# Clock products from a constant, and two products moved ahead of a wait: the two ends of a TensorE-bound cross network

## The chip, the cores and the metric

One core of a Trainium2 chip. The metric is the device time of one execution in microseconds. Most numbers below are of two kinds: the **time** of a run, and the **span** that the profile of one execution shows from first to last instruction.

## The reference, cut to what matters

```
B, F, D, L = 16384, 26, 16, 6          # Din = 416
x = x0
for l in range(L):
    proj = einsum('bd,de->be', x, ws[l]) + bs[l]
    x = x0 * proj + x                   # x0 [16384, 416], ws [6, 416, 416], all bf16
```

## The kernel before

The rows are in 8 groups of 2048. A group lies in SBUF transposed, features on partitions: three tiles of 128 features and a tail of 32. TensorE multiplies, ScalarE takes the sum out of PSUM and adds the bias (L398), VectorE multiplies by x0 (L407) and adds x (L412). A helper `add` records every operation with what it reads and writes and sets semaphores from that; each engine's list is in the order of the calls.

Ahead of the first data, products that nobody reads keep TensorE busy. They are there to have its clock open sooner: in e5, without them, it opened at 9.34 us, in the profile of after at 4.54. I call them clock products, and 128 columns of one a unit:

```
def keep_busy(n, b):
    while n > 0:
        m = min(n, 4)
        add("pe", lambda h, m=m: h.matmul(
            bank(b, n=m * P).rearrange("p (m c) -> p m c", m=m), ones[:, :],
            ones[:, :].unsqueeze(1).broadcast_to([P, m, P]), start=True, stop=True),
            reads=["ones"], writes=[("ps", b)])
        n -= m
keep_busy(22, 7)          # before the first transposes
...                       # keep_busy(2, 3) between them, keep_busy(5, 3) after them
```

The last job (last group, last layer) works with rows on partitions, so that its output can be stored as it is: four row blocks kk, each of four chunks j, each chunk three products of 416 columns (`nat_full`, L868), one product of the 32-row tail (`nat_rows`, L912) and one of the bias (L917). ScalarE copies a chunk out (L923), VectorE multiplies (L929) and adds the residual (L935), and one store per block goes out. The residual of the last tile is still being made when this starts, and TensorE transposes it (`turn_last`, L879):

```
a0, a1, a2, a3 = bka = take(NJ)
b0, b1, b2, b3 = take(NJ)
bks = {0: bka, 1: [b0, b3, b1, a0], 2: [a1, a2, a3, b2], 3: [b0, b3, b1, a0]}
store(LAST - 1, 0, 2)                  # output of the last but one group,
store(LAST - 1, 2, NJ)                 # two stores of 832 KB
for j in range(NJ):
    nat_full(0, j, bks[0][j], True, (0, 1))
turn_tails(b0)
nat_rows(0, bks[0], False)
turn_last(0, b1)
turned_out(0, b1)
for j in range(NJ):
    if j == 2:
        turn_last(2, b2)
    nat_full(0, j, bks[0][j], False, (2,))
    nat_out(0, j, bks[0])
...
for kk in range(1, KK):
    nat_rows(kk, bks[kk])
    for j in range(NJ):
        nat_full(kk, j, bks[kk][j], False)
        nat_out(kk, j, bks[kk])
        ...                            # nat_mul, nat_add on VectorE, nat_store
```

## Time and profile before

| | before |
|---|---|
| time, median of 3 runs | 475.43 us (475.24 to 475.45) |
| time and span of the profiled run | 477.81 us, 476.0 us |
| TensorE busy | 470.3 us (99%) |
| first real product | 6.46 us |
| last store issued | 473.58 us |

The prediction shows the lines of the page, of the chain and of the timeline.

### The profile page before, as it was taken

To read this page: it belongs to the slowest core of one execution; us is meant where nothing else is said; L and a number is where in the kernel's file an instruction comes from. 1 tells how busy PE (TensorE), PEld (TensorE's weight loads), DVE (VectorE), ACT (ScalarE), POOL (GpSimd) and SP (SyncE) were. 2 spreads that over 40 slices of the span, in tenths; PEclk is the share of its full clock that TensorE was granted. 3 is DMA by queue.
4 is the path that set the end of the run, shared out by engine and by line. 5 is a ranking of instruction groups with operands and counts; after the bars stand their busy time and mean duration, and the time that the engine had idled before them with its cause. 6 is when DMAs were issued, how large, how long until landed. Compare 5 with 4: busy or idle time off the path is not lost.

```text
span 476.0 us, 8464 instructions
## 1 busy us (share of the span) xinstructions
PE 470.3 (99%) x3407; PEld 200.9 (42%) x3407; DVE 404.2 (85%) x699; ACT 342.0 (72%) x372; POOL 6.3 (1%) x15
## 2 busy tenths in 40 slices
PE   8999999999999999999999999999999999999996
PEld 4434444654444444444444444444444444444442
DVE  1798888888888888898889869988888888888897
ACT  3677777777777777777777777777777777777776
POOL 1000000000000000000000000000000000001000
PEclk9999999999999999999999999999999999999999
DMA  8986830650001398469409940890001029125899
GB/s 223 171 173 143 185 88 1 110 113 1 19 16 30 65 240 147 67 134 239 111 12 170 240 102 10 175 289 2 1 1 35 0 56 232 34 45 101 222 175 288
DMA packets 138651, 53.18 MB, mean 112 GB/s; under 512 B 112362, under 2 KB 138100, under 8 KB 138612
## 3 DMA queue, kind: packets, MB, share of 16 engines
q1 hardware_dynamic: 138456, 52.54, 49.9%
q8 instruction: 26, 0.43, 0.4%
q14 instruction: 13, 0.11, 0.1%
q10 hardware_dynamic: 156, 0.11, 0.1%
HBM read 5.97 MB, written 13.63 MB: 41 GB/s over the span
## 4 chain that ended last, share of the span: by engine, by line
PE 96%; DMA 2%; ACT 1%; DVE 1%; SPq 0%; issue 0%; DVEq 0%
PE ps L471 78%; PE ps L492 7%; PE ps L513 7%; PE ps L868 1%; PE ps L486 1%; DMA wm<-in_ws_dram 1%; ACT tw L398 1%; PE ps L504 1%; PE ps L592 1%; DMA ot<-x 1%; DVE tw L407 0%; PE ps L879 0%; ACT x L923 0%; DVE x L929 0%; DVE x L935 0%; PE ps L912 0%
## 5 line engine op out<-in xcount | busy, mean ns | idle before, releaser
L398 ACT ACTIVATE tw<-ps,bias 128x1024 bf16<-128x1024 f32 (+1 forms) x295 | 299.8, 1071 | 119.5 <-PE ps L492 81.1
L471 PE MATMUL ps<-x,wm 128*128 128x512 bf16 (+1 forms) x1755 | 380.9, 373 | 0.5 <-DMA wm<-in_ws_dram 0.5
L471 PEld LDWEIGHTS ps<-x,wm 128*128 128x128 bf16 x1755 | 165.3, 98 | 210.0 <-issue 29.3
L407 DVE TENSOR_TENSOR tw<-tw,x 128x1024 bf16<-128x1024 bf16 (+1 forms) x285 | 192.7, 684 | 51.8 <-ACT tw L398 51.2
L412 DVE TENSOR_TENSOR x<-tw,x 128x1024 bf16<-128x1024 bf16 (+1 forms) x285 | 182.6, 681 | 0.0
L492 PE MATMUL ps<-x,w 32*128 32x512 bf16 x512 | 39.2, 379 | 0.0
L513 PE MATMUL ps<-x,wm 128*32 128x512 bf16 x564 | 33.0, 380 | 0.0
L438 ACT ACTIVATE ts<-ps,bias 128x512 bf16<-128x512 f32 x47 | 28.8, 701 | 0.0
L442 DVE TENSOR_TENSOR x<-ts,x 128x512 bf16<-128x512 bf16 x47 | 18.7, 419 | 3.9 <-DMA x<-x 3.8
L513 PEld LDWEIGHTS ps<-x,wm 128*32 128x32 bf16 x564 | 13.8, 96 | 17.6 <-issue 5.3
L492 PEld LDWEIGHTS ps<-x,w 32*128 32x128 bf16 x512 | 7.8, 92 | 26.9 <-issue 26.4
L440 DVE TENSOR_TENSOR ts<-ts,x 128x512 bf16<-128x512 bf16 x47 | 18.6, 419 | 0.0
L602 DVE COPY x<-ps 128x512 bf16<-128x512 bf16 x5 | 2.0, 423 | 10.7 <-PE ps L592 10.7
L712 POOL COPY ost<-ot 128x512 bf16<-128x512 bf16 x6 | 4.8, 805 | 424.3 <-DMA ot<-x 424.3
L868 PE MATMUL ps<-wm,x 128*128 128x416 bf16 x48 | 9.5, 340 | 0.0
L604 ACT ACTIVATE x<-ps 128x512 bf16<-128x512 bf16 x7 | 3.8, 595 | 7.4 <-PE ps L592 7.4
L923 ACT ACTIVATE x<-ps 128x416 bf16<-128x416 f32 x16 | 7.8, 526 | 1.6 <-PE ps L868 1.5
L868 PEld LDWEIGHTS ps<-wm,x 128*128 128x128 bf16 x48 | 4.3, 98 | 4.2 <-issue 1.0
L504 PE MATMUL ps<-x,w 32*32 32x512 bf16 x188 | 5.9, 374 | 0.0
L486 PE MATMUL ps<-x,w 32*32 32x512 bf16 x208 | 5.6, 385 | 0.0
L929 DVE TENSOR_TENSOR x<-x,x 128x832 bf16<-128x832 bf16 (+1 forms) x10 | 4.9, 502 | 0.6 <-ACT x L923 0.4
L935 DVE TENSOR_TENSOR x<-x,x 128x832 bf16<-128x832 bf16 (+1 forms) x9 | 4.7, 540 | 0.2
(41 smaller groups left out, 35.4 us busy)
## 6 DMA issues: line engine op xcount, KB each, us to landing
out_dram<-ost SPq DMA_DIRECT2D x6, 1664.0 KB, 7.0
x<-x SPq DMA_DIRECT2D x24, 96.0 KB, 2.1
wm<-in_ws_dram SPq DMA_DIRECT2D x6, 312.0 KB, 3.4
x<-in_x_dram SPq DMA_DIRECT2D x8, 208.0 KB, 4.8
x<-in_x_dram SPq DMA_DIRECT2D x4, 416.0 KB, 8.3
out_dram<-ost SPq DMA_DIRECT2D x2, 832.0 KB, 5.5
x<-x SPq DMA_DIRECT2D x22, 64.0 KB, 2.0
out_dram<-x SPq DMA_DIRECT2D x3, 416.0 KB, 4.1
```

Source lines behind the costliest of these rows:

```text
L398: add("act", lambda h, a=a, w=w, b0=b0: h.activation(tw[r][:, a * CH:(a + w) * CH], psum[:, b0 * CH:(b0 + w) * CH], ACT_F.Identity, bias=b ...
L407: add("dve", lambda h, a=a, e=e: h.tensor_tensor(tw[r][:, a * CH:e * CH], tw[r][:, a * CH:e * CH], x0s[s0][:, i * GC + a * CH:i * GC + e * ...
L412: add("dve", lambda h, a=a, e=e: h.tensor_tensor(xs[so][:, i * GC + a * CH:i * GC + e * CH], tw[r][:, a * CH:e * CH], src(i, a, e), ALU.ad ...
L438: add("act", lambda h: h.activation(ts[r][:, :], bank(b), ACT_F.Identity, bias=bias[:, 3, l:l + 1], scale=1.0), reads=[("ps", b), "bias"], ...
L440: add("dve", lambda h: h.tensor_tensor(ts[r][:, :], ts[r][:, :], x03, ALU.mult), reads=[("ts", r)] + tok0, writes=[("ts", r)], release=True)
L442: add("dve", lambda h: h.tensor_tensor(x3s[so][:, :], ts[r][:, :], res, ALU.add), reads=[("ts", r)] + rtok, writes=[("x3", so), ("x3", so, ...
L471: add("pe", lambda h, t=t, j=j, k=k, w=w: h.matmul(bank(banks[j])[:, k * w:(k + 1) * w], wm[l][:, t, ecols], src(t, j, j + 1)[:, k * w:(k ...
L486: add("pe", lambda h, q=q, j=j, r=r, c=c, o=o: h.matmul(psum[o, banks[j] * CH:(banks[j] + 1) * CH], w3[l][q, i * P + c * T32:i * P + (c + ...
L492: add("pe", lambda h, q=q, j=j, r=r: h.matmul(bank(banks[j]), w3[l][q, ecols], src[q, :], start=first and not inner, stop=not first and no ...
L504: add("pe", lambda h, l=l, b=b, s3=s3, ri=ri, qi=qi, ro=ro, qo=qo: h.matmul(psum[qo, b * CH:(b + 1) * CH], w3[l][qi, NT * P:D], s3[qi, :], ...
L513: add("pe", lambda h, t=t, j=j, src=src, l=l, b=b, ro=ro, qo=qo: h.matmul(psum[qo, b * CH:(b + 1) * CH], wm[l][:, t, NT * P:D], src(t, j, ...
L868: add("pe", lambda h, t=t: h.matmul(bank(b, n=D), xcol(t, j, kk), wm[l][:, t, :], start=(first and t == 0), stop=(not first and t == NT - 1)),
```

## The change

The intent: begin the clock products sooner, by reading a constant that is written at 0.30 us, before the queues begin at 0.73 to 0.80, instead of a tile that GpSimd must fill first (0.73 to 0.93 us), and use the time gained for three more units; and use the wait for the last residual tile for two products of the second row block.

```
 def keep_busy(n, b):
+    one = nc.const_aps.tensor(1.0, [P, CH], BF16)
     while n > 0:
         m = min(n, 4)
         add("pe", lambda h, m=m: h.matmul(
-            bank(b, n=m * P).rearrange("p (m c) -> p m c", m=m), ones[:, :],
-            ones[:, :].unsqueeze(1).broadcast_to([P, m, P]), start=True, stop=True),
-            reads=["ones"], writes=[("ps", b)])
+            bank(b, n=m * P), one[:, 0:P], one[:, 0:m * P], start=True, stop=True), writes=[("ps", b)])
         n -= m
-keep_busy(22, 7)
+keep_busy(25, 7)
...
 nat_rows(0, bks[0], False)
+nat_full(1, 1, bks[1][1], True, (0, 1))
 turn_last(0, b1)
...
 for kk in range(1, KK):
-    nat_rows(kk, bks[kk])
+    begun = (1,) if kk == 1 else ()
+    nat_rows(kk, bks[kk], begun=begun)     # no fresh start for a chunk that has begun
     for j in range(NJ):
-        nat_full(kk, j, bks[kk][j], False)
+        nat_full(kk, j, bks[kk][j], False, (2,) if j in begun else range(NT))
```

More of the change, by code (lines that the diff above doesn't have):

```diff
@@ L907, in turn_tails, with nat_rows @@
             j += n
-    def nat_rows(kk, bks, first=True):
+    def nat_rows(kk, bks, first=True, begun=()):
         for j in range(NJ):
@@ L912, in nat_rows @@
             add("pe", lambda h, j=j, q=q, r=r: h.matmul(
-                bank(bks[j], n=D), x3col(j, kk), w3[l][q, :], start=first, stop=False, tile_position=(r * T32, 0)),
+                bank(bks[j], n=D), x3col(j, kk), w3[l][q, :], start=first and j not in begun, stop=False, tile_position=(r * T32, 0)),
                 reads=tok3 + [("w3", l, r)], writes=[("ps", bks[j])])
```

## The prediction

The clock estimate: that the doubling stays at 10.3 us, worth 0, against rival 1 (20%), that it comes at about 6.9 us, for a time of about 474. The 6.9 us is 10.28 less 3.41 us. The forecast's sum is 475.43 - 0.1 (tail) - 0 (head) = 475.33 us, less some 0.2 for the 20% of a gain near 1.2, so 475.2, in a range of 474.2 to 475.6.

> **What bounds the kernel now.** I read the page's busy shares, then the chain that ended last, then the timeline of the first 13 us and of the last 17 us, because the change touches only those two ends.
>
> ```profile
> PE 470.3 (99%) x3407; PEld 200.9 (42%) x3407; DVE 404.2 (85%) x699; ACT 342.0 (72%) x372; POOL 6.3 (1%) x15
> PE 96%; DMA 2%; ACT 1%; DVE 1%; SPq 0%; issue 0%; DVEq 0%
> ```
>
> TensorE sets the pace: 99% busy and 96% of the chain. The change removes no product between 14 and 459 us, so it can only move the two ends. The start of the chain, in order of time (start, duration, what):
>
> ```profile
> 1.65 4.67 DMA wm<-in_ws_dram
> 6.33 0.14 issue
> 6.46 2.72 PE ps L471 x6
> 9.18 1.97 PE ps L592 x24
> 11.16 1.29 PE ps L471 x6
> ```
>
> The first real products wait for the first weight matrix, which lands at 6.32 us. Six products of 512 columns then take 2.72 us (453 ns each), the next six 1.29 us (215 ns each): TensorE ran at half rate first. The 24 transposes of 128 columns between them take 1.97 us; 12 at about 107 ns and 12 at about 56 ns give that, so the rate doubled at about 10.3 us (estimate: 8.97 us, the first transpose, plus 12 x 0.107). The row of granted clock shows 9 in every slice and does not show this. The clock products (the page's L572) stand ahead of it:
>
> ```profile
> 0.73 0.20 POOL L522 MEMSET ones<- 128x128 bf16 x1 [0.29 <-POOLq L1003]
> 0.98 0.13 PEld L572 LDWEIGHTS ps<-ones 128*128 128x128 bf16 x2 [0.98 <-POOL ones L522]
> 0.99 2.53 PE L572 MATMUL ps<-ones 128*128 128x512 bf16 x6 [0.99 <-POOL ones L522]
> 3.37 0.56 PEld L592 LDWEIGHTS ps<-ident,x 128*128 128x128 bf16 x6 [0.55 <-DMA x<-in_x_dram]
> ```
>
> They wait for the memset of ones (0.73 to 0.93) and end as the first rows land. At the tail, VectorE:
>
> ```profile
> 461.94 0.42 DVE L407 TENSOR_TENSOR tw<-tw,x 128x512 bf16<-128x512 bf16 x1
> 462.28 0.75 DVE L412 TENSOR_TENSOR x<-tw,x 128x512 bf16<-128x512 bf16 x2
> 466.39 0.59 DVE L929 TENSOR_TENSOR x<-x,x 128x832 bf16<-128x832 bf16 x1
> 467.02 0.59 DVE L935 TENSOR_TENSOR x<-x,x 128x832 bf16<-128x832 bf16 x1
> 467.53 0.59 DVE L929 TENSOR_TENSOR x<-x,x 128x832 bf16<-128x832 bf16 x1
> 468.15 0.59 DVE L935 TENSOR_TENSOR x<-x,x 128x832 bf16<-128x832 bf16 x1
> ```
>
> The chain calls the tail TensorE's, but here VectorE runs nearly without a gap from 466.39 us on: starts lie 0.63, 0.51, 0.62 and 0.58 us apart while one operation lasts 0.59. That matters below.
>
> [...]I expect no slower weight load (0.15 us now); this trace does not show it.
>
> **The change part by part.**
>
> *Clock products, start.* The constant is written at 0.30 us, before the start barrier; the other queues begin at 0.73 to 0.80 us. So I put the first product at about 0.75 instead of 0.99: 0.24 us earlier. *Clock products, number.* 25 units of 128 columns instead of 22. A 512-column product starts every 0.427 us (weight loads at 1.39, 1.82, 2.24, 2.67), so a unit is 0.107 us: 25 x 0.107 = 2.67, end 0.75 + 2.67 = 3.42 us; before, 0.99 + 22 x 0.107 = 3.34. The first transposes move from 3.37 to about 3.42. They are off the path: the weights land at 6.32 whatever happens. Direct worth: 0.
>
> *The clock.* [...] So most probably the doubling stays at 10.3 us and is worth 0. If it did come at 6.9 us: of six products from 6.46, one is cold and five run at 0.216, saving about 5 x 0.21 = 1.05 us; 12 cold transposes save 12 x 0.051 = 0.6. The sum 1.65 us is an upper estimate, since the rows of the later chunks are still landing until about 8.5 us and the copies out of PSUM lie between.
>
> *The tail.* Two products of the second row block (bank b3) move ahead of the transposes. Bank b3 is the last tile's own fourth bank: ScalarE frees it only when its fourth eviction (L398, four from 459.31, 2.41 us long) ends at 461.72. On TensorE, the rows' products issue at 461.33; in the later row blocks the next full product follows 0.28 us after them with nothing to wait for (463.95 to 464.23). So the transposes at 461.61 were not late at all, though the profile puts 0.34 us of idle to the add before them. The true gap is from 461.61 + 4 x 0.056 = 461.83 to 462.08 (0.25 us, the add of the second chunk), and another before 462.75.
>
> Worked forward: pair at 461.77 and 461.95 (0.176 us apart: 12 of them start over 1.94 us, 11 steps); eight transposes 462.13 to 462.58; two products to 462.95; transposes of chunks 2 and 3 (data at 462.75 and 463.08) at 462.95 and 463.17; last two products from 463.41 instead of 463.32. So block 0 ends 0.09 us **later**: of 0.35 us put in, 0.26 fell into gaps. Block 1 then has 10 full products instead of 12: 0.35 us off. Net for TensorE, 0.26 us earlier into blocks 2 and 3.
>
> *What follows it.* ScalarE: block 0's third copy-out starts 0.37 us after its product, 463.69 now, 463.80 after; then the fourth, the 1.03 us copy of the turned chunks (464.51) and block 1's two, all back to back; so VectorE's multiply at 466.39 moves to about 466.49. From there VectorE needs 0.63 + 0.51 us per pair. Seven more starts (0.63, 0.51, 0.62, 0.51, 0.62, 0.51, 0.62) and 0.51 to the next put the first single multiply of the last block at 466.49 + 4.53 = 471.02, where it starts at 470.99 now. The second single multiply starts at 471.41 now, waiting for ScalarE's copy that begins at 470.86; that copy now comes 0.26 us earlier, so it follows at about 471.33. The rest hangs on it: 0.08 us earlier. **Sum of the tail: about 0.1 us gained**, against 0.35 us of product time moved.
>
> **The rivals.**
>
> 1. [...] 20%.
> 2. *TensorE alone sets the tail*: then 0.26 us would be gained, 475.15. For: the chain's tail is mostly PE L868. Against: VectorE's gapless starts.
> 3. *The wait for bank b3 takes the place of the wait for the tile*: if the transposes are held longer than I worked out, every later copy slips, and the end comes up to 0.2 us later, 475.6. For: the bank is freed 0.11 us after the point where TensorE wanted to go on. Against: the gaps at 461.83 and 462.4 absorb most.
> 4. *Broadcast reads are slow or upset the clock*[...]. Nothing in the profile speaks for it; the ones tile held the same values. 3%.
>
> **Range and chances.** The main path is 475.43 - 0.1 = 475.33. Weighing in 20% for a gain near 1.2 us takes off some 0.2 in the mean; I say 475.2. The three runs before spread over 0.21 us, so the upper end is 475.6; the lower end 474.2 holds part of the clock's case. Two per cent is 9.5 us, more than five times the largest effect here, so "within 2%" is nearly certain.
>
> **What would show it.** Right: the first clock product at about 0.75 us; the first weight product still at 6.46, the six products from there still 2.7 us; the moved pair at about 461.77, released by ScalarE's L398; block 0's last pair about 0.1 us later; block 1 with 10 products; VectorE without gaps from 466.5 us, and the end some 0.1 us earlier. Wrong: if the 24 transposes or the six products take half, the clock opened earlier, and the gain is over 1 us; if VectorE shows waits for ScalarE through blocks 2 and 3, TensorE led and the gain is 0.26; if the moved pair starts after 462.0, it costs.

## The result, and the profile after

| | before | after |
|---|---|---|
| median of 6 runs in the same rounds | 475.44 us (475.13 to 476.41) | 475.75 us (475.00 to 477.76) |
| ratio, 95% interval | | 1.0009 (0.9989 to 1.0029) |
| span of the profiled run | 476.0 us | 473.7 us |

Ratios here are the mean time of one kernel's runs over that of the other's of the same rounds, so not quite the ratio of the medians. The median lies 0.15 us above my range. And the two spans say the opposite of the two medians: the profiled run of after is 2.3 us **shorter**.

The page of after, the line of busy time and the chain's shares by engine:

```profile
PE 462.3 (98%) x3354; PEld 200.1 (42%) x3408; DVE 404.1 (85%) x699; ACT 341.9 (72%) x372; POOL 6.1 (1%) x15
PE 93%; ACT 3%; DVE 2%; issue 1%; DMA 1%; DVEq 0%
```

TensorE lists fewer products (3354) than before (3407) although the change removes none: a trace can miss some, and the busy sum with them. So I go by positions in time. The timeline of the start after (start, length, engine, line):

```profile
0.77 2.83 PE L573 MATMUL ps<-const-bfloat16-1.0 128*128 128x512 bf16 x7 [0.77 <-PEq L1004]
3.39 0.85 PE L591 MATMUL ps<-ident,x 128*128 128x128 bf16 x6
...
4.24 0.65 PE L591 MATMUL ps<-ident,x 128*128 128x128 bf16 x6
...
6.06 1.46 PE L471 MATMUL ps<-x,wm 128*128 128x512 bf16 x6 [0.52 <-ACT x L603]
```

The products start at 0.77 as intended. The second group of six transposes takes 0.65 us instead of 0.85, so the clock opened in the middle of it, at about 4.5 us (on record 4.54), and the first six real products take 1.46 us where the profile before had 2.72. The first real product also starts sooner, at 6.06 us instead of 6.46. That looks like a gain of two microseconds, and by the prediction's own signs of being wrong it would be one of over 1 us; the timed runs show none of it. Either something gives it back, or the two profiles are not of the same kind of run.

The tail after, VectorE and the moved pair (L867 here is L868 before):

```profile
459.66 0.53 PE L867 MATMUL ps<-wm,x 128*128 128x416 bf16 x2 [0.26 <-ACT tw L398]
...
464.36 0.59 DVE L928 TENSOR_TENSOR x<-x,x 128x832 bf16<-128x832 bf16 x1
464.98 0.59 DVE L934 TENSOR_TENSOR x<-x,x 128x832 bf16<-128x832 bf16 x1
465.49 0.58 DVE L928 TENSOR_TENSOR x<-x,x 128x832 bf16<-128x832 bf16 x1
466.11 0.59 DVE L934 TENSOR_TENSOR x<-x,x 128x832 bf16<-128x832 bf16 x1
```

The pair waits 0.26 us for ScalarE's last eviction, and VectorE then runs without gaps, at steps of 0.62 and 0.51 us up to the single operations of the last block, as predicted. The tail is measured below from ScalarE's copy (L710, after: L709) to the issue of the last store; before and after:

```profile
458.78 0.63 ACT L710 ACTIVATE ost<-ot 128x512 bf16<-128x512 bf16 x1 [0.57 <-DMA ot<-x]
473.58 0.38 ACTq L942 DMA_DIRECT2D out_dram<-x  x1
```

```profile
456.66 0.63 ACT L709 ACTIVATE ost<-ot 128x512 bf16<-128x512 bf16 x1 [0.73 <-DMA ot<-x]
471.33 0.38 ACTq L941 DMA_DIRECT2D out_dram<-x  x1
```

473.58 - 458.78 = 14.80 us and 471.33 - 456.66 = 14.67 us: the last store is issued 0.13 us sooner.

### The profile page after: what moved, and what is told of

Its sections match the earlier page's. It is cut to its first block, busy times and chain, and to the rows that moved or that the text cites. A ratio compares the mean times of both kernels' runs of the same rounds, so it can differ in the third digit from the quotient of the medians.

```text
span 473.7 us, 8412 instructions
## 1 busy us (share of the span) xinstructions
PE 462.3 (98%) x3354; PEld 200.1 (42%) x3408; DVE 404.1 (85%) x699; ACT 341.9 (72%) x372; POOL 6.1 (1%) x15
## 4 chain that ended last, share of the span: by engine, by line
PE 93%; ACT 3%; DVE 2%; issue 1%; DMA 1%; DVEq 0%
PE ps L471 77%; PE ps L492 7%; PE ps L513 6%; ACT tw L398 2%; PE ps L486 1%; DVE x L928 1%; DVE x L934 1%; PE ps L573 1%; PE ps L504 1%; ACT x L922 1%; DMA ot<-x 1%; PE ps L591 0%; ACT x L603 0%; ACT x L888 0%; DVE x L601 0%
## 5 line engine op out<-in xcount | busy, mean ns | idle before, releaser
L471 PE MATMUL ps<-x,wm 128*128 128x512 bf16 (+1 forms) x1701 | 372.1, 371 | 6.1 <-issue 3.7
L492 PE MATMUL ps<-x,w 32*128 32x512 bf16 x512 | 39.2, 379 | 0.0
L492 PEld LDWEIGHTS ps<-x,w 32*128 32x128 bf16 x512 | 7.8, 92 | 26.9 <-issue 26.4
L867 PE MATMUL ps<-wm,x 128*128 128x416 bf16 x48 | 9.7, 340 | 0.3 <-ACT tw L398 0.3
L867 PEld LDWEIGHTS ps<-wm,x 128*128 128x128 bf16 x48 | 4.2, 98 | 4.8 <-issue 1.0
```

The lines of the kernel that those rows point to most:

```text
L471: add("pe", lambda h, t=t, j=j, k=k, w=w: h.matmul(bank(banks[j])[:, k * w:(k + 1) * w], wm[l][:, t, ecols], src(t, j, j + 1)[:, k * w:(k ...
L492: add("pe", lambda h, q=q, j=j, r=r: h.matmul(bank(banks[j]), w3[l][q, ecols], src[q, :], start=first and not inner, stop=not first and no ...
L867: add("pe", lambda h, t=t: h.matmul(bank(b, n=D), xcol(t, j, kk), wm[l][:, t, :], start=(first and t == 0), stop=(not first and t == NT - 1)),
```

## The experiments

Sixteen runs were made (e1 is the kernel before, e2 and e12 are the changed kernel). Theory one: both kernels have early and late runs, by when the clock opens; the change gains a tenth in the tail and the first medians are scatter. Rivals: one of the two parts costs 0.3 us.

### 1 to 4: both kernels again, and each part alone (one chip)

Edits: none; none (changed kernel); the `keep_busy` part of the diff alone; the `nat_full` part alone.

> The kernel before, unchanged, against itself. Theory (two kinds of run): the profiled run of before (477.81 us, span 476.0) was of a late kind in which TensorE's clock opened at about 10.3 us; its timed runs at 475.4 were of an early kind. So times cluster at 475.2 to 475.6 with a rare 477.5 to 478, ratio 1.000, and a profile that falls in the early kind shows a span near 473.6 and the first six weight products in about 1.5 us, not 2.7. Rival (the profile alone is slow): all profiles have a span of 476 and six products in 2.7 us, whatever the timed runs say.

> The changed kernel again. Theory (two kinds, tail worth 0.1): fast kind at 475.3 to 475.6, ratio to before 0.9995 to 1.0000 where both are of the early kind; a late run now and then near 477.8. Rival (the change costs): 475.7 to 475.9 again, ratio 1.0005 to 1.0010 in runs of the early kind.

> Only the clock products' part of the change (constant source, 25 units). Theory: in runs of the early kind nothing, 475.4, ratio 1.0000 within 0.0005; only the share of late runs may change. Rival (the head costs): 475.8, ratio 1.0008, because the first transposes start later or the clock opens later in the typical run.

> Only the two moved products. Theory: 0.1 us less than before, 475.3, with VectorE gapless from the first multiply of the second row block on. Rival (TensorE leads): 475.15. Rival (the moved pair holds up the transposes): 475.6 or more.

| | median, us | lowest to highest | span of the profile |
|---|---|---|---|
| kernel before in the same rounds (11 runs) | 476.03 | 475.25 to 477.65 | |
| e1_before (6) | 475.67 | 475.60 to 475.98 | 473.9 |
| e2_after (7) | 475.51 | 475.39 to 478.24 | 476.4 |
| e3_head (6) | 475.76 | 475.60 to 477.56 | 473.9 |
| e4_tail (6) | 475.70 | 475.43 to 476.65 | 473.8 |

All four ratios have intervals that include 1; the upper ends are 1.0001 (e2) to 1.0014 (e3). Taken alone, the medians of e1, e3 and e4 lie above what I had expected and those of e3 and e4 near their rivals' numbers, but so does the kernel before in the same rounds, at 476.03; the ratios, 0.9984 to 0.9995, speak for no loss. Now it is the kernel before that has the short profile and the changed kernel the long one. The start of the kernel before in the run e1:

```profile
4.17 0.72 PE L592 MATMUL ps<-ident,x 128*128 128x128 bf16 x6
...
5.65 1.46 PE L471 MATMUL ps<-x,wm 128*128 128x512 bf16 x6
```

The kernel before has an early kind too, with the clock open before the first weights (six products in 1.46 us). And the changed kernel in the run e2, a late one:

```profile
3.39 0.51 PE L591 MATMUL ps<-ident,x 128*128 128x128 bf16 x6
...
4.55 0.45 PE L573 MATMUL ps<-const-bfloat16-1.0 128*128 128x512 bf16 x2
...
7.08 2.72 PE L471 MATMUL ps<-x,wm 128*128 128x512 bf16 x6 [2.08 <-DMA wm<-in_ws_dram]
```

Six transposes in 0.51 us: here the clock was open at 3.4 us already, earlier than in any other profile. Then the weights came late, TensorE stood idle for 2.08 us, and the six real products ran at half rate again (2.72 us, in e1 1.46): the clock had closed. So a late run comes about in two ways, by opening late (the profile before) or by opening early and closing in the wait.

The kept traces also record when the granted clock changed. `prof e2_after --windows` gives its mean over a stretch (the number before the last two):

```profile
3.40:6.80 3.40, 1.60 (x24) 1.00 0.98 272
6.90:10.20 3.30, 3.12 (x12) 0.50 1.25 260
10.30:13.00 2.70, 2.63 (x33) 1.00 0.91 187
```

By the record the clock of e2 was full from 3.40 to 6.82 us, at half to 10.23 us, and full again: two steps of 3.41 us. In the records of the first two profiles the time from the first opening to the last closing is 464.21 us (before) and 467.63 us (after), 136.0 and 137.0 times 3.413 us. So in these three profiles the changes of the clock lie whole steps of 3.41 us apart. The first opening came at 3.40 to 5.44 us in 15 profiles and at 9.34 to 10.38 us in three (before, e5, e12): the steps do not begin with the kernel, and the three with the later opening are late runs. The clock is not all of the scatter: the first real product began between 5.65 us (e1) and 7.08 us (e2), mostly as the weights landed, and that moves early runs too.

What this settles: the 2.3 us between the first two profiles are not the change's. The rival that a part costs 0.3 us is not borne out in these rounds: the whole change is at 475.51 us in the median, the kernel before at 476.03.

### 5 to 7: take the clock products away, fill the wait, move a copy

e5 takes all clock products out of the changed kernel; e6 fills the wait for the weights; e7 moves the copy (L709) that ScalarE does ahead of the last tile's evictions.

```
e5:  +    n = 0                     # in keep_busy
e6:  -    keep_busy(5, 3)           +    keep_busy(14, 3)
e7:  -    spread("act")             +    spread("pool")
```

> The changed kernel with every clock product taken out (results unchanged). Theory (the time's scatter is the clock's opening): nothing keeps TensorE busy before the first weights at about 6.1 us, so the clock opens only around 10 us or later in every run: all runs of the late kind, 477.5 to 478.5, none near 475.5; the profile shows the first six weight products in 2.7 us. Rival (the clock products do not matter, the late kind is something else): the same mix as the changed kernel, mostly 475.5.

> The changed kernel with 14 units instead of 5 in the last group of clock products, so that TensorE idles less before the first weights (one profile of the changed kernel had the clock open at 3.4 us and closed again in 2.1 us of waiting for the weights). Theory: early runs unchanged at 475.5, within 0.1; no late run near 478, or fewer. Rival (more clock products only delay): all runs 0.3 to 1 us later.

> The changed kernel with the copy that waits for a DMA ahead of the last tile's evictions moved from ScalarE to GpSimd. ScalarE idles 0.6 to 0.8 us there and then copies for 0.63 us. If ScalarE held up the tail: about 1 us less. My reading: VectorE is the one that is nearly full there (its last tile's operations start at once after the tile before), so only some 0.2 us: 475.3 in early runs, and the stretch from the last tile's first eviction to the last store's issue changes accordingly. Rival: GpSimd's copy slows VectorE's operations beside it, and nothing or a loss comes out.

| | median, us | lowest to highest | ratio, 95% interval |
|---|---|---|---|
| kernel before in the same rounds (9) | 475.99 | 475.67 to 476.56 | |
| e5_noclock (5) | 477.90 | 476.85 to 478.46 | 1.0037 (1.0024 to 1.0051) |
| e6_bridge (5) | 475.60 | 475.35 to 475.91 | 0.9990 (0.9978 to 1.0003) |
| e7_pool (5) | 475.56 | 475.50 to 475.65 | 0.9989 (0.9977 to 1.0002) |

Without clock products TensorE's start is, in its profile:

```profile
3.37 1.56 PE L592 MATMUL ps<-ident,x 128*128 128x128 bf16 x12 [3.37 <-DMA x<-in_x_dram]
...
5.72 2.72 PE L471 MATMUL ps<-x,wm 128*128 128x512 bf16 x6 [0.51 <-DMA wm<-in_ws_dram]
```

The six products are at half rate. The fastest of the five runs is 0.3 us above the slowest of the kernel before, and the medians are 1.9 us apart. Two runs, 476.85 and 477.00, are below the 477.5 I had expected. The first of them is the profiled one: its clock opened at 9.34 us (10.38 in the profile before), and its weights let TensorE start at 5.72 us (6.46). The clock's opening does make most of the late kind, and the clock products of either kernel buy about 2 us in most runs. For e6, five runs are too few to say that late runs are gone.

e7 met its rival. The two additions of the tile before the last took 1.29 us in the changed kernel and, beside GpSimd's copy, this long in e7 (the first line is the changed kernel's):

```profile
456.57 1.29 DVE L412 TENSOR_TENSOR x<-tw,x 128x1024 bf16<-128x1024 bf16 x2
456.39 1.70 DVE L412 TENSOR_TENSOR x<-tw,x 128x1024 bf16<-128x1024 bf16 x2
```

GpSimd's copy began at 456.55 and showed 1.00 us, so it ran beside these additions, which took 0.41 us longer than without it; by what mechanism, no trace shows. So, it seems, VectorE gave back what ScalarE gained: from the last tile's row products (L492) to the last store's issue e7 takes 17.18 us and the changed kernel 17.19.

### 8 and 9: is it VectorE that keeps half of the tail's gain?

In both kernels without the additions of row blocks 1 and 2 (wrong result):

```
             elif j % 2:
                 nat_mul(kk, j - 1)
-                nat_add(kk, j - 1)
```

> Wrong result on purpose: the kernel before without the additions of row blocks 1 and 2, so that VectorE has room in the tail. From the ScalarE copy ahead of the last tile's evictions to the issue of the last store the kernel before takes 14.80 us and the changed one 14.67 in every profile. Theory (VectorE takes over the tail): here TensorE leads, and this stretch stays near 14.75 to 14.80 since TensorE led it before too.

> Wrong result on purpose: the changed kernel without the additions of row blocks 1 and 2. Theory (VectorE takes over the tail and keeps half of the gain): the stretch from the ScalarE copy ahead of the last tile's evictions to the issue of the last store falls to about 14.5, that is 0.25 to 0.3 below the same edit of the kernel before, instead of 0.13 below. Rival (the waiting pair costs the other half, VectorE is innocent): the difference stays 0.13.

The measure is again the stretch from ScalarE's copy ahead of the last evictions to the issue of the last store (ACTq). The two ran on different chips. It is steadier than any time: 14.80 us in all three profiles with the old tail and complete work (before, e1, e3), 14.67 in all six with the new one (after, e2, e4, e5, e6, e12). Without the additions, before and after:

```profile
457.22 0.63 ACT L710 ACTIVATE ost<-ot 128x512 bf16<-128x512 bf16 x1 [0.76 <-DMA ot<-x]
472.03 0.38 ACTq L942 DMA_DIRECT2D out_dram<-x  x1
```

```profile
457.22 0.63 ACT L709 ACTIVATE ost<-ot 128x512 bf16<-128x512 bf16 x1 [0.65 <-DMA ot<-x]
471.73 0.38 ACTq L941 DMA_DIRECT2D out_dram<-x  x1
```

472.03 - 457.22 = 14.81 and 471.73 - 457.22 = 14.51: 0.30 us apart instead of 0.13. So VectorE does keep the other 0.17 us, as predicted. But look at the ends: from the copy to the end of the span both take 17.18 us (474.4 - 457.22). The last store leaves 0.30 us earlier, and the program ends at the same moment. That was not in any of my theories.

### 10 to 12: a later copy, and the changed kernel a third time

e10 puts the copy (L709) and the two 832 KB stores after `turn_tails`, where ScalarE idles; e11 has the 14 units of e6 too; e12 is the changed kernel.

```
-                spread("act")                 # in the loop over tiles
...
-store(LAST - 1, 0, 2)
-store(LAST - 1, 2, NJ)
 for j in range(NJ):
     nat_full(0, j, bks[0][j], True, (0, 1))
 turn_tails(b0)
+spread("act")
+store(LAST - 1, 0, 2)
+store(LAST - 1, 2, NJ)
```

> The changed kernel with the ScalarE copy that waits for a DMA put after the last tile's evictions and the tails' copies, where ScalarE idles 0.69 us, instead of ahead of the evictions. Moved to GpSimd it had slowed VectorE's additions (1.63 us for two instead of 1.29) and gained nothing. Expected: from the last tile's row products on TensorE (L492) to the issue of the last store 16.9 to 17.0 us instead of 17.12 to 17.20; bank b3 is free sooner, so the moved pair waits less; early runs at 475.3. Rival (VectorE's last-tile operations are full already): 17.15, nothing gained.

> The same with 14 units in the last group of clock products too. Expected: as the one before in early runs, 475.3 to 475.4, and no run above 476.2; the kernel before in the same rounds at 475.4 to 476.5 with a stray 477.5.

> The changed kernel a third time, for the share of late runs and its distance to the kernel before on another chip. Theory (0.13 us in the tail, the rest is when the clock opens): early runs within 0.4 us of early runs of before, mean difference -0.1 to -0.3, ratio 0.999 to 1.000; the first session's +0.3 does not come back. Rival (a real loss of 0.3): 1.0006 or more.

| | median, us | lowest to highest | L492 to last issue | last issue to end |
|---|---|---|---|---|
| kernel before in the same rounds (11) | 475.70 | 475.30 to 478.35 | | |
| e10_late (6) | 475.75 | 475.36 to 476.01 | 16.86 | 2.8 |
| e11_best (6) | 475.99 | 475.37 to 476.32 | 16.87 | 2.9 |
| e12_after (6) | 477.06 | 475.50 to 477.97 | 17.14 | 2.5 |

e10 issues its last store 0.3 us sooner, as expected, and ends no sooner: what it gained comes back between the last issue and the end. Its median, 475.75, is not the 475.3 I had expected. e11 gained nothing either, and its slowest run, 476.32, is above the 476.2 I had allowed. e12 had three late runs of six and a ratio of 1.0019 (0.9996 to 1.0043); its profile is a late one with the first six products in 2.72 us. My expectation of 0.999 to 1.000 failed there, and the ratio is as high as the rival of a real loss had it (1.0006 or more). Its other three runs are at 475.50, 475.66 and 476.54, so the excess is in the late ones; whether their number is chance stays open.

The transfers explain the tail. In the profile of e10, from 455 to 474 us in 40 slices, the rate moved:

```profile
GB/s 168 188 84 43 216 206 147 212 200 177 218 192 167 209 184 341 361 298 356 342 340 343 329 343 338 317 342 329 331 335 331 328 328 333 336 321 182 11 0 0
```

About 1 us after the issue of the first output store (461.11) the rate rises, and it stays at 298 to 361 GB/s, mostly 320 to 345, until 472.1 us: 3.3 MB of output, half of it of the last but one group, in some 10 us. Whether this rate is a limit, the trace does not show. And in all fourteen profiles up to here, from the issue of the first of these stores to the end of the span it takes 12.73 to 12.91 us, whatever the kernel did in between, while the time from that issue to the last one ranged from 9.97 (e10) to 10.48 (before).

### 13 to 16: is it the drain of the stores?

e13 and e14 leave out the second 832 KB store in the kernel before and in the changed kernel (wrong result); e15 and e16 issue the first from ScalarE's queue after `turn_tails`, in the changed kernel and in e10.

```
e13, e14:  -store(LAST - 1, 2, NJ)
e15, e16:  -store(LAST - 1, 0, 2)      +store(LAST - 1, 0, 2, "act")   # after turn_tails (and spread)
```

> Wrong result on purpose: the kernel before without the second of the two 832 KB stores of the last but one group. Theory (the drain of the stores sets the end): the stretch from the ScalarE copy ahead of the last tile's evictions to the end of the span falls from 17.2 to about 16.8 us, and the time from the last store's issue to the end from 2.3 to 2.4 to about 2.0. Rival (fixed landing time): that time stays 2.3 to 2.4.

> Wrong result on purpose: the changed kernel without that store. Theory (drain): from the ScalarE copy to the end 0.13 us (0.1 to 0.2) less than in the same edit of the kernel before, where the two full kernels differ by 0.02 on average. Rival: they end alike here too.

> The changed kernel with the first half of the last but one group's output stored from ScalarE's queue after the tails' copies, about 460.2 us in place of 461.0 in the first profile's time. Theory (drain): the stores begin 0.7 us earlier and the end comes 0.3 to 0.4 us earlier, to what the last store's own issue and landing allow; from the last tile's row products (L492) to the end 19.2 to 19.4 us, where all profiles so far show 19.54 to 19.74. Rival (the end is not the drain's): 19.6, nothing gained.

> The same with the late ScalarE copy of e10, whose last store is issued 0.3 us earlier but gained nothing. Theory: from L492 to the end 19.0 to 19.3 us; early runs some 0.3 to 0.5 us below the kernel before in the same rounds. Rival: 19.6.

| from ScalarE's copy (L710, L709) | to the last issue, old tail / new | to the end of the span, old tail / new |
|---|---|---|
| complete work (mean of before, e1, e3 / of after, e2, e4, e5, e6, e12) | 14.80 / 14.67 | 17.17 / 17.15 |
| additions left out (e8 / e9) | 14.81 / 14.51 | 17.18 / 17.18 |
| one big store left out (e13 / e14) | 14.81 / 14.67 | 17.02 / 16.91 |

Spans are read to 0.1 us, so a single one of the last column can be off by 0.05. The packed traces hold the spans to the nanosecond; with them the last column reads 17.20 / 17.15, 17.13 / 17.15 and 17.06 / 16.91. With the store left out, the end comes earlier in both kernels, and the 0.14 us of the last issue shows in the end as 0.11 (0.15 by the finer spans, one profile each). The stretch to the end in e13 is 17.02 us, where I had expected about 16.8, and from last issue to end it is 2.2 us in both, where I had expected 2.0; so about 2.2 is what a last store takes with a freer queue, and the drain costs only some 0.2 us more. The three stores of 416 KB before it land 2.7 us after issue in e13 and e14; in the two complete kernels it was 4.1 and 3.9. The lists of transfers say the same of the last store, from issue to landing: with VectorE relieved 1.8 us in the kernel before and 2.1 in the changed one, so the 0.3 us was waited out in the queue; with the store left out 1.8 in both:

```profile
out_dram<-x ACTq DMA_DIRECT2D x1, 104.0 KB, 2.1
```

```profile
out_dram<-x ACTq DMA_DIRECT2D x1, 104.0 KB, 1.8
```

The first is e9, the second e14. The drain theory holds, in size less than I had expected.

The cure did not. e15 is at 476.91 us (476.72 to 477.56) with the kernel before at 475.76: ratio 1.0026 (1.0014 to 1.0039); e16 at 477.25, ratio 1.0041 (1.0027 to 1.0055). In e15 VectorE shows why:

```profile
465.40 0.59 DVE L934 TENSOR_TENSOR x<-x,x 128x832 bf16<-128x832 bf16 x1 [1.82 <-DMA x<-x]
```

ScalarE came by the store at 458.97 us, between the issues of the two transposing transfers (458.0 and 459.3) that turn the residual for that addition. The first landed 3.2 us after issue, as in the changed kernel; the second took 5.9 us instead of 3.3, and VectorE waited 1.82 us. In e16 the store is issued at 460.23, after both (458.1 and 459.4), and still one of them took 6.2 us and VectorE waited 2.16 us. So in both, with a store sent early, a transfer that the computation needs took 5.9 and 6.2 us instead of 3.3. No version here beats both kernels.

## Why the prediction was wrong

**What held.** The class, within 2%, which was nearly certain. The clock product at 0.75 (0.77), its end at 3.42 (transposes at 3.39), no direct worth of the head. The weight loads from the constant no slower (137 ns in the mean, before 138). The moved pair released by ScalarE, its wait, and VectorE without gaps from block 1 on; the last store's issue 0.13 us earlier where I had 0.08 to 0.1. Rival 2 (0.26 us if TensorE led) is answered by e8 and e9: with VectorE relieved it is 0.30, so VectorE was the right reading. Rivals 3 and 4 are not borne out. The first real product came at 6.06 us in the first profile after, not at 6.46.

**The step that failed first: "So most probably the doubling stays at 10.3 us and is worth 0", and with it the upper end "475.6" from a spread of 0.21 us over three runs.** I read the state of the clock from one profiled run and the width from three timed ones, and the two were of different kinds: the profiled run took 477.81 us, the others 475.43. In the early kind the clock is open before the weights land in both kernels (e1: six products in 1.46 us). So the opening at 10.3 us is no property of the kernel before, and the 2.3 us that the first profile of after seemed to show are no gain of rival 1.

The comparison under it failed too: it took TensorE's busy share over stretches of 3.41 us as what tells whether the clock opens. Counted back from the recorded opening at 10.38 us, TensorE of the kernel before was busy for 2.57, 2.93 and 3.41 of 3.41 us, and the clock was not open after the first two. In e7, which has the new head, the stretch at almost the same place as the first had 2.78 us, and the clock opened at its end (PEclk reads 1.00 before the first opening because the record begins there):

```profile
0.15:3.56 3.41, 2.57 (x8) 1.00 0.46 136
3.56:6.97 3.41, 2.93 (x24) 1.00 0.97 293
```

```profile
0.14:3.55 3.41, 2.78 (x9) 1.00 0.48 131
```

e15 did the same (2.79 us, open at 3.56). So 2.93 us went without an opening and 2.78 with one, and the busy share alone was no measure. In these two profiles the clock with the new head did open earlier than in the first profile of before, as rival 1 had it; that the head did it is not shown. It does not show in the median, because 50 of 53 timed runs of the kernel before are early ones without it; its clock opened at 4.62 us in e1.

What the medians show instead is two kernels alike. Over all rounds (without the profiled run of 477.81) the kernel before was timed 53 times, at 475.13 to 478.35 us with a median of 475.75; the changed kernel 19 times, at 475.00 to 478.24 with a median of 475.72. The median after that put me outside the range, 475.75, is that same number: the three runs I started from lay 0.3 us below the kernel's own middle, and the range had no room for it.

**The term that was mis-sized: "about 0.1 us gained".** The last issue does come 0.13 us earlier, but the end is set by the output stores draining, so next to nothing of it arrives: 17.15 against 17.17 us (17.20 by the finer spans, within their scatter of 0.15). My sum stopped at VectorE and took the time after the last issue as fixed. It is 2.3 to 2.4 us with the old tail, 2.4 to 2.6 with the new, 2.7 to 2.9 where the tail is faster still, and 2.2 with a freer queue.

**What stays open.** Whether the head changes the share of late runs. The changed kernel had 5 late runs of 19, the kernel before 3 of 53 (4 of 54 with its profiled run), which looks like a loss; but the other five timed kernels with the new head and all stores on SyncE's queue but the last (e3, e6, e7, e10, e11) had 1 of 28. They are not the same kernels, two of them fill the wait, and these runs don't decide it. The mean granted clock on record is a hint: it is 0.994 or 0.995 in three of the changed kernel's five late runs, e2's profile among them, and in one of the four of the kernel before; the others have 0.998 or 0.999. So the changed kernel's late runs may be more often of the kind that opens early and closes in the wait. What sets where the steps of 3.41 us fall, and what opens the clock at the end of one and not of another, is not shown.

## What to carry to other kernels

Before reading a profile, hold its own time against the timed runs: if they differ by more than the spread, the profile may be of another kind of run, and what it shows at the differing place isn't what the median pays for. A range cannot be narrower than the scatter of the kernel it starts from, and three runs do not show that. And follow a gain through to the last byte: here it passed TensorE, ScalarE and VectorE and was lost in a full store queue, which only a look at issue-to-end, not at the engines, could show.

## What else the traces show

- The clock closed in a gap of TensorE of 2.08 us (e2: six transposes in 0.51 us before it, six products in 2.72 us after it; TensorE was busy for 1.60 of the 3.40 us from 3.40 to 6.80). After a gap of 1.27 us in e9 it was open (six products in 1.45 us).
- Six transposes took 0.82 to 0.85 us at the low rate and 0.50 to 0.51 at the high one, so an open clock speeds them up. What they do for an opening is not shown: after a stretch of 3.41 us that was about half of transposes, with 2.93 us busy, the clock was not open (before), after one with 2.78 it was (e7), and so it was after one busy throughout, with fewer clock products than the latter (e4, open at 5.20).
- The opening varies from run to run: with gaps between the first products the clock of one kernel was open by 3.40 us in one run (e2) and not until 9.78 in another (e12). The spans of the first two profiles, which opened at 10.38 and 4.54 us, are 2.3 us apart (476.0 against 473.7; 0.4 of it is the start of the first real product): half a per cent, and larger than the change measured here.
- A store's issue-to-end time hid gains of the engines: it went from 2.2 us with one big store left out (e13, e14) to 2.9 with all stores and an earlier issue (e11), while the drain moved 298 to 361 GB/s, mostly 320 to 345 (e10).
- The row of granted clock in the profile shows 9 in the first slice also where products take twice as long (453 and 215 ns): a trace's record begins with the first opening (10.38 us in the profile before), and what lies before it counts as full. Where the clock closed again, in e2, the first slice shows 8.
